# The output projection as a part of its own behind attention, by seven products for two row tiles, with contexts and gate through DRAM

## The chip, the core and the metric

The kernel runs on one core of one Trainium2 chip. The metric is the device time of one execution in microseconds, as the median of several runs. One more execution is recorded by the hardware profiler; its page and its trace give the durations used here. Engines are named as the profile names them: PE (matmul), PEld (weight loads of the matmuls), DVE (vector), ACT (scalar), POOL (GpSimd), SP (the queue that issues nearly all DMAs). "L738" is line 738 of the kernel.

## The reference, cut to what matters

```
x  = A_x                      # 1 x 2048 x 640, bfloat16
xn = layernorm(x)
q  = xn @ wq                  # 640 -> 32 heads x 192
k, v = the last 512 of 2048 cached positions, per head
o  = softmax(q k^T / sqrt(192)) @ v          # 32 heads, 2048 queries, 512 keys
s  = concat(o) @ wo           # 6144 -> 640
g  = silu((silu(xn @ w_gate) * (xn @ w_up)) @ w_down)   # 640 -> 1536 -> 640
out = x + s * g
```

Everything is bfloat16 in DRAM. There is no mask.

## The kernel before, in words

**Tiling.** The 2048 rows are 16 row tiles of 128, or 4 blocks of 512 (`NB`). Two heads make a pair (`NPAIR` = 16 pairs), 384 wide, which is three slices of 128. One (pair, block) is a step `i = pr * NB + b`. The order on every engine is written out by hand (the pools run under `manual_schedule`), so each engine executes its instructions in the order of the program, and a waiting instruction holds up all that stands behind it on its engine.

**First part.** Layernorm, and the gate branch (`ffn_hidden`, `ffn_down`), whose result `g` stays in SBUF in two layouts: columns 0 to 511 by row (`g_m`), columns 512 to 639 transposed (`g_t`). `x_transpose` keeps the same columns of x transposed in `xT`.

**Attention, pair by pair.** For each pair there are two halves of two blocks each. A half is a scores phase and a stretch.
- `scores_phase(pr, half)` has eight slots n. In each, `scores` makes S = k q for 128 keys, 512 queries and two heads (six matmuls of 64 rows by 512 columns; two row groups of 64 run side by side) and ACT takes the exponential (L601). Between them stand the products that make the q of a later half (`q_group`: `differences` at n = 0, `sides` at 1, `across` and `third(0)` at 3, `sums` at 4, `third(1)` at 6). `across` is a DVE instruction (L576) that must have read the PSUM tile before the matmuls of `sums` may add to it.
- `beside(pr, n)` puts loads and K work next to slot n, with n counted from 0 to 15 over both halves: `transpose_k(pr+1, kc)` (DMA transposes of the next pair's K, L167) at n = 0 to 3, `load_v(pr)` at 0, `load_wo(pr)` at 4, `sum_k` (DVE reductions over those transposes, L174) at 8 to 10, `load_k(pr+2)` at 11, `centre_k` at 12 to 15, `load_wq(pr+2)` at 15.
- The stretch multiplies the exponentials with V: `pv(i, q2)`, two units ("0a0" is block 0, rows 0 to 255, first turn) of 16 matmuls of 64 by 193 columns; between the two turns of one accumulator POOL writes a tiny tile (L725) that the second turn waits for. `divide` normalises the accumulators into `O_b` (DVE and ACT), and a DMA transpose (L655) turns `O_b` into `OT_b`, the context with its features on the partitions.
- Between the units of a stretch stand the output projection's units of the half before (`wo_units`): `wo_turn` (L738), row-tiled matmuls of 64 by 512 for columns 0 to 511, and `rest` (through `wo_rest`, L708) for columns 512 to 639 transposed. DVE adds each result to the running sums `s_m` and `s_t` in SBUF (`add_sum`, L751). So each pair's 384 features are projected as they come. The orders are three strings: `FIRST` (no projection yet), `LATER` and `LAST`.

**Pairs 14 and 15.** POOL multiplies the sums with g and adds x (L767, L778). Two of the four blocks of pair 14 are held back and projected together with pair 15's (`late`), and the last rows are finished in small pieces (`last_rows`, `wo_parts`, L833, L834) and stored.

**DMA.** SP issues in program order into one queue. Nothing that attention makes goes to DRAM before the output itself.

Of the kernel before, what the change touches and what calls it, by code (L numbers as in the profile page):

```python
# [15 lines left out]
def kernel(  # L16
# [34 lines left out]
    MC = D - P  # L51
# [14 lines left out]
    res = ctx.enter_context(tc.tile_pool(name="res", bufs=1))  # L66
    wpool = ctx.enter_context(tc.tile_pool(name="att_w", bufs=2))
    kpool = ctx.enter_context(tc.tile_pool(name="att_k", bufs=1))
    qpool = ctx.enter_context(tc.tile_pool(name="att_q", bufs=2))
    sc_pool = ctx.enter_context(tc.tile_pool(name="psum_sc", bufs=2, space=bass.MemoryType.PSUM))  # L70
# [14 lines left out]
    g_m = res.tile([P, T, MC], bf, name="g_m")  # L85
    g_t = res.tile([P, NB, 512], bf, name="g_t")
    xT = res.tile([P, NB, 512], bf, name="xT")

    NG = NB // 2
    DIFF, SUM, DIAG = 0, NG, 2 * NG  # L90
    xc = res.tile([P, 2 * NG + 1, NC, 512], h16, name="xc")

# [9 lines left out]
    V_p = consts.tile([P, KC, 2, Dh + 8], bf, name="V_p")  # L102
# [49 lines left out]
    def load_wo(pr):  # L152
        wo_p = pairs[pr]["wo"] = wpool.tile([P, 3, D], bf, name="wo_p")
        nc.sync.dma_start(
            out=wo_p[:], in_=wo[pr * PD : (pr + 1) * PD, :].rearrange("(j p) d -> p j d", p=P)
        )

# [40 lines left out]
    with ExitStack() as fctx:  # L201
        ffw = fctx.enter_context(tc.tile_pool(name="ffw", bufs=1))
        lnw = fctx.enter_context(tc.tile_pool(name="lnw", bufs=4))
        lnx = fctx.enter_context(tc.tile_pool(name="lnx", bufs=8))
        ffh = fctx.enter_context(tc.tile_pool(name="ffh", bufs=2))
        ffa = fctx.enter_context(tc.tile_pool(name="ffa", bufs=3))
# [124 lines left out]
        def x_transpose(t):  # L331
            nc.sync.dma_start_transpose(
                out=xT[:, t // 4, (t % 4) * P : (t % 4 + 1) * P], in_=x_t[t][:, MC:D]
            )

        def ffn_down(b, u):

            dn = mm_tile()[:, 0, :]
            to = g_m[:, 4 * b + u, :] if u < 4 else g_t[:, b, :]
            for f in range(NF):  # L340
                if u < 4:
                    at, by = hTs[b][:, f, u * P : (u + 1) * P], wd_sb[:, f, 0:MC]
                else:
                    at, by = wd_sb[:, f, MC:D], hTs[b][:, f, :]
                nc.tensor.matmul(dn, at, by, start=(f == 0), stop=(f == NF - 1))  # L345
            nc.scalar.activation(to, dn, ACT.Silu)
# [88 lines left out]
        mm_pool.append(ctx.enter_context(tc.tile_pool(name="psum_mm", bufs=1, space=bass.MemoryType.PSUM)))  # L435
# [4 lines left out]
        for b in range(NB):  # L440
# [4 lines left out]
            for f in range(NF):  # L445
# [13 lines left out]
                if f >= 8:  # L459
                    x_transpose(4 * b + f - 8)  # L460
# [17 lines left out]
                if b >= 1 and f in (1, 4, 6, 9, 11):  # L478
                    ffn_down(b - 1, u)
                    u += 1  # L480
                if b == 2:
                    if f == 0:
                        load_k(0)
                    elif 2 <= f < 6:
                        transpose_k(0, f - 2)
                    elif f == 6:
                        load_wq(0)
                    elif 7 <= f < 10:
                        sum_k(0, f - 7)
                elif b == 3:  # L490
                    if f < 5:
                        centre_k(0, f)
                    elif f < 8:
                        (load_k, load_wq, load_wo)[f - 5]((1, 1, 0)[f - 5])
        early_q = [(i, j) for i in range(2) for j in range(3)]
        for u in range(5):
            ffn_down(NB - 1, u)
            for _ in range((0, 1, 2, 2, 1)[u]):
                q_full(*early_q.pop(0))
            if xwork:  # L500
                xwork.pop(0)()
# [3 lines left out]
    sapool = ctx.enter_context(tc.tile_pool(name="sacc", bufs=1))  # L505
    ppool = ctx.enter_context(tc.tile_pool(name="att_p", bufs=10))
    opool = ctx.enter_context(tc.tile_pool(name="att_o", bufs=2))
    otpool = ctx.enter_context(tc.tile_pool(name="att_ot", bufs=3))
    smpool = ctx.enter_context(tc.tile_pool(name="att_sm", bufs=8))
    finp = ctx.enter_context(tc.tile_pool(name="fin", bufs=2))  # L510
    s_m = sapool.tile([P, T, MC], f32, name="s_m")
    s_t = sapool.tile([P, NB, 512], f32, name="s_t")
    m_f = sapool.tile([P, 2, 2, 512], f32, name="m_f")

    NS = NPAIR * NB
    turn_t = smpool.tile([P, 1], f32, name="turn_t", bufs=1)
    last = NPAIR - 1
    Ps, OTs, Obs, xbs = {}, {}, {}, {}


# [83 lines left out]
    def pv(i, q2):  # L604

        pr, b = divmod(i, NB)
        st = {}

        def part(p):
            if p == 0:  # L610
                if i not in OTs:
                    Obs[i] = opool.tile([P, 4, 2, Dh], bf, name="O_b")
                    tag = "OT_l" if late(i) and pr < last else "OT_b"
                    OTs[i] = otpool.tile([P, 12, P], bf, name=tag, tag=tag, bufs=2 if tag == "OT_l" else 3)
                st["acc"] = sc_tile() if i < 2 and q2 else mm_tile()
# [15 lines left out]
            if p == 3:  # L631
                divide(i, q2, acc, (0, 1) if q2 == i else (0,) if pr == last else ())
# [3 lines left out]
    def divide(i, q2, acc, by_dve):  # L636
        pr, b = divmod(i, NB)
# [4 lines left out]
        for k in range(2):  # L642
            qt = 2 * q2 + k
            a_k = a_v[:, k, :, :]
            if by_dve and k in by_dve:
# [14 lines left out]
    def pv_full(i, q2):  # L660

        pr, b = divmod(i, NB)
        if i not in OTs:
            Obs[i] = opool.tile([P, 4, 2, Dh], bf, name="O_b")
            tag = "OT_l" if late(i) and pr < last else "OT_b"
            OTs[i] = otpool.tile([P, 12, P], bf, name=tag, tag=tag, bufs=2 if tag == "OT_l" else 3)
        O_b, OT_b = Obs[i], OTs[i]
        acc = mm_tile()
        for k in range(2):
            qt = 2 * q2 + k  # L670
            for h in range(2):
                for kc in range(KC):
                    nc.tensor.matmul(  # L673
                        acc[:, k, h * 256 : h * 256 + Dh + 1],
                        Ps[i][kc][:, h, qt * P : (qt + 1) * P], V_p[:, kc, h, 0 : Dh + 1],
                        start=(kc == 0), stop=(kc == KC - 1),
                    )
        divide(i, q2, acc, ())

    def load_xb(b):  # L680

        xbs[b] = xc[:, (SUM, DIFF + 1, DIAG, DIFF)[b], :, :].rearrange("p c n -> p (c n)").bitcast(bf).rearrange(
            "p (t d) -> p t d", d=D
        )
        nc.sync.dma_start(
            out=xbs[b][:, :, MAIN],
            in_=x2[b * 512 : (b + 1) * 512, MAIN].rearrange("(t p) d -> p t d", p=P),
        )

    def rows(b, qts):  # L690

        t = slice(4 * b + qts.start, 4 * b + qts.stop)
        return s_m[:, t, :], g_m[:, t, :]

    def late(i):
        return i // NB >= NPAIR - 2 and i % NB >= 2

    def wo_cols(ps, i, qt, cols, first=True, end=True):
        for j in range(3):
            nc.tensor.matmul(  # L700
                ps, OTs[i][:, 3 * qt + j, :], pairs[i // NB]["wo"][:, j, cols],
                start=(first and j == 0), stop=(end and j == 2),
            )

    def wo_rest(ps, i, r=slice(0, P), first=True, end=True):

        for j in range(3):
            nc.tensor.matmul(  # L708
                ps.rearrange("p (t q) -> p t q", q=P), pairs[i // NB]["wo"][r, j, MC:D],
                OTs[i][:, :, :].rearrange("p (t j) q -> p j t q", j=3)[r, j, :, :],  # L710
                start=(first and j == 0), stop=(end and j == 2),
            )

    MAIN = slice(0, MC)

    def follows(m, earlier):
        tc.add_manual_dep(
            m.ins, earlier.ins.name,
            mybir.DependencyInfo(mybir.DependencyClass.Sync, mybir.DependencyReason.DATA),
            reason="row tiles change banks",  # L720
        )

    def turned(m, st):

        st["turn"] = nc.gpsimd.memset(turn_t[:], 0.0)  # L725
        follows(st["turn"], m)

    def after(m, st):
        if "turn" in st:
            follows(m, st.pop("turn"))  # L730

    def wo_turn(st, i, half, turn):

        ps = st["sc"]
        for j in range(3):
            for n, r in enumerate((lo, hi)):
                k = n ^ turn
                m = nc.tensor.matmul(  # L738
                    ps[:, k, :], OTs[i][r, 3 * (2 * half + k) + j, :],
                    pairs[i // NB]["wo"][r, j, MAIN],  # L740
                    start=(turn == 0 and j == 0), stop=(turn == 1 and j == 2), skip_group_check=True,
                )
                after(m, st)
        if turn == 0:
            turned(m, st)

    def add_sum(pr, to, ps):
        if pr == 0:
            nc.vector.tensor_copy(out=to, in_=ps)
        else:  # L750
            nc.vector.tensor_tensor(to, to, ps, ALU.add)  # L751

    def sum_rows(i, qts, sc):
        pr, b = divmod(i, NB)
# [272 lines left out]
```

## Time and profile before

| | |
|---|---|
| median of 3 runs | 912.74 us (912.26 to 912.97) |
| the profiled execution | 913.02 us, of which its instructions span 911.2 us |
| PE, DVE, ACT, POOL busy | 902.4, 585.6, 501.2, 149.0 us |
| granted PE clock | 1.000 |
| matmuls of the output projection | L738 x1296, L708 x354, L700 x144 |
| DMA | 81.98 MB, mean 90 GB/s |

The profile gives for each engine its busy time, and for each group of instructions of one line and shape their number, their busy time and the mean of one. Matmuls are pipelined: a matmul's "mean" is its way through the array, and what it costs in a row of others is the distance between two starts, which the timeline shows. A chain of waits is followed back from the last instruction: it says which engine was the limit in each stretch of time.

### The profile page before, as it was taken

The page shows a single profiled execution, that of the slowest core. Times are in us where ns is not written, and L with a number is a line of the kernel's source. Part 1 is how long each engine was busy: PE and PEld are TensorE (multiplying, and loading weights), DVE is VectorE, ACT ScalarE, POOL GpSimd, SP SyncE. Part 2 cuts the span into 40 slices and gives each one's busy share as a digit, 9 for nine tenths or more (in the row PEclk, how much of TensorE's full clock was granted, in tenths as well). Part 3 has the DMA queues.
Part 4 walks back from the last instruction along what each step waited for, and adds up shares of the span by engine and source line. Part 5 has one row for each costly group of instructions (what it writes and reads, how often), then busy time and mean ns, then how long its engine had stood idle before and what let it go on. Part 6 is the DMA issues. An engine that isn't in the chain of part 4 may idle for free.

```text
span 911.2 us, 23325 instructions
## 1 busy us (share of the span) xinstructions
PE 902.4 (99%) x9835; PEld 543.1 (60%) x9835; DVE 585.6 (64%) x862; ACT 501.2 (55%) x873; POOL 149.0 (16%) x299
## 2 busy tenths in 40 slices
PE   9999999999999999999999999999999999999988
PEld 5444444466666666666666666666666666665555
DVE  5443553365767676767676767676776767676767
ACT  4222222566656666666666666666565656565671
POOL 0000000011111111111111111111111111116746
PEclk9999999999999999999999999999999999999999
DMA  9414360044544544454445444444544554454435
GB/s 300 82 33 95 76 142 5 1 83 92 82 93 83 92 83 92 82 92 79 97 77 97 79 96 76 80 97 81 88 83 92 78 92 86 91 78 110 120 46 165
DMA packets 266025, 81.98 MB, mean 90 GB/s; under 512 B 244928, under 2 KB 265920, under 8 KB 265920
## 3 DMA queue, kind: packets, MB, share of 16 engines
q1 hardware_dynamic: 263552, 77.82, 43.5%
q10 hardware_dynamic: 2368, 2.67, 0.9%
q8 instruction: 77, 1.26, 0.6%
q14 instruction: 28, 0.23, 0.1%
HBM read 41.39 MB, written 2.62 MB: 48 GB/s over the span
## 4 chain that ended last, share of the span: by engine, by line
PE 94%; POOL 3%; issue 1%; DMA 1%; DVE 1%; ACT 0%; ACTq 0%; POOLq 0%
PE mm L622 17%; PE sc L597 16%; PE sc L738 15%; PE mm L543 12%; PE sc L315 11%; PE mm L529 7%; PE mm L345 6%; PE sc L708 4%; PE sc L700 2%; POOL s_m L778 1%; PE mm L673 1%; POOL s_m L767 1%; PE mm L700 1%; PE mm L352 1%; DMA x_t<-in_A_x_dram 1%
## 5 line engine op out<-in xcount | busy, mean ns | idle before, releaser
L601 ACT ACTIVATE p_t<-sc 128x1024 bf16<-128x1024 f32 x256 | 253.8, 1024 | 81.9 <-PE sc L597 81.7
L652 ACT ACTIVATE O_b<-mm,r 128x192 bf16<-128x192 f32 x490 | 166.0, 421 | 184.0 <-issue 110.4
L597 PE MATMUL sc<-qT,khat 64*128 64x512 bf16 x1536 | 197.6, 376 | 0.0
L622 PEld LDWEIGHTS <-p_t 64*128 64x128 bf16 x3744 | 166.4, 94 | 39.9 <-issue 2.9
L622 PE MATMUL mm<-V_p,p_t 64*128 64x193 bf16 x3680 | 186.9, 243 | 2.1 <-ACT O_b L652 1.1
L751 DVE TENSOR_TENSOR s_m<-s_m,sc 128x1024 f32<-128x1024 f32 x108 | 131.9, 1221 | 60.7 <-PE sc L738 52.9
L738 PE MATMUL sc<-wo_p,OT_b 64*128 64x512 bf16 x1296 | 169.1, 376 | 0.0
L597 PEld LDWEIGHTS <-khat 64*128 64x128 bf16 x1536 | 88.4, 94 | 75.7
L534 DVE TENSOR_REDUCE qT<-mm 128x512 bf16<-128x1024 f32 x66 | 80.8, 1224 | 32.8 <-PE mm L529 29.9
L751 DVE TENSOR_TENSOR s_t<-s_t,sc 128x512 f32<-128x512 f32 x108 | 74.2, 687 | 40.4 <-PE sc L708 38.5
L725 POOL MEMSET turn_t<- 128x1 f32 x225 | 22.1, 98 | 467.1 <-PE mm L622 282.4
L738 PEld LDWEIGHTS <-OT_b 64*128 64x128 bf16 x1296 | 70.3, 94 | 44.4 <-issue 0.3
L581 POOL TENSOR_TENSOR m_f<-m_f 128x1024 f32<-128x1024 f32 x28 | 65.7, 2348 | 177.8 <-DVE qT L576 171.5
L543 PE MATMUL mm<-xc,wq_p 64*128 64x512 f16 x750 | 94.4, 376 | 0.0
L543 PEld LDWEIGHTS <-wq_p 64*128 64x128 f16 (+1 forms) x1050 | 58.7, 94 | 54.5 <-issue 0.8
L529 PE MATMUL mm<-xnT,wq_p 64*128 64x512 bf16 x660 | 82.9, 376 | 1.0 <-DVE qT L534 0.9
L323 DVE TENSOR_TENSOR hT<-sc,sg 128x512 bf16<-128x512 f32 x46 | 31.7, 691 | 70.2 <-ACT sg L322 70.2
L322 ACT ACTIVATE sg<-sc 128x512 bf16<-128x512 f32 x46 | 27.3, 596 | 69.8 <-PE sc L315 69.8
L315 PE MATMUL sc<-xnT,wg_sb 128*128 128x512 bf16 (+1 forms) x260 | 60.3, 354 | 0.4 <-DMA wg_sb<-in_B_w_gate_dram 0.3
L576 DVE TENSOR_TENSOR qT<-mm,m_f 128x1024 bf16<-128x1024 f32 x30 | 36.7, 1224 | 37.2 <-ACT m_f L573 37.2
L315 PE MATMUL sc<-xnT,wu_sb 128*128 128x512 bf16 (+1 forms) x260 | 60.3, 355 | 0.3 <-DMA wu_sb<-in_B_w_up_dram 0.3
L529 PEld LDWEIGHTS <-wq_p 64*128 64x128 bf16 x660 | 36.0, 94 | 37.9 <-issue 6.5
(96 smaller groups left out, 717.1 us busy)
## 6 DMA issues: line engine op xcount, KB each, us to landing
wo_p<-in_A_wo_dram SPq DMA_DIRECT2D x16, 480.0 KB, 3.9
wq_p<-in_A_wq_dram SPq DMA_DIRECT2D x79, 80.0 KB, 2.9
K_p<-in_A_k_cache_dram SPq DMA_DIRECT2D x32, 192.0 KB, 3.0
V_p<-in_A_v_cache_dram SPq DMA_DIRECT2D x32, 192.0 KB, 3.1
wq_p<-in_A_wq_dram SPq DMA_DIRECT2D x90, 40.0 KB, 2.7
x_t<-in_A_x_dram SPq DMA_DIRECT2D x13, 160.0 KB, 3.0
xc<-in_A_x_dram SPq DMA_DIRECT2D x4, 512.0 KB, 4.1
OT_b<-O_b SPq DMA_TRANSPOSE x124, 2.8
```

Source lines behind the costliest of these rows:

```text
L315: nc.tensor.matmul(out, w_sb[:, c, f * P : (f + 1) * P], xnT[:, c, qc], start=(c == 0), stop=(c == NC - 1),)
L345: nc.tensor.matmul(dn, at, by, start=(f == 0), stop=(f == NF - 1))
L529: nc.tensor.matmul(q_ps[:, h, :], w[r, AS_IS[j], c, :], xnT[r, c, b * 512 : (b + 1) * 512], start=(c == 0), stop=(c == NC - 1),)
L534: nc.vector.reduce_sum(q_of(i, j), q_ps[:, :, :].rearrange("p h n -> p n h"), axis=AX.X)
L543: nc.tensor.matmul(ps[:, h, :], ws[h][r, c, :], xs[h][r, c, :], start=(first and c == 0), stop=(c == NC - 1), skip_group_check=True,)
L581: eng.tensor_tensor(m_f[:, SIDE_S, :, :], diag, m_f[:, SIDE_S, :, :], ALU.subtract)
L597: nc.tensor.matmul(sc[:, h, :], khat[r, j, ks], q_of(i, j)[r, :], start=(j == 0), stop=(j == 2))
L601: nc.scalar.activation(p_t[:, :, :], sc[:, :, :], ACT.Exp, scale=scale)
L622: m = nc.tensor.matmul(acc[:, k, h * 256 : h * 256 + Dh + 1], Ps[i][kc][r, h, qt * P : (qt + 1) * P], V_p[r, kc, h, 0 : Dh + 1], start=(p ...
L652: nc.scalar.activation(O_b[:, qt, h, :], a_k[:, h, 0:Dh], ACT.Copy, scale=r[:, k, h, :])
L738: m = nc.tensor.matmul(ps[:, k, :], OTs[i][r, 3 * (2 * half + k) + j, :], pairs[i // NB]["wo"][r, j, MAIN], start=(turn == 0 and j == 0), ...
L751: nc.vector.tensor_tensor(to, to, ps, ALU.add)
```

## The change

- The running sums, `wo_units`, `LATER` and all of the output projection inside attention are gone. A stretch now holds the V units alone (`CONTEXTS`, the order that `FIRST` was), with "a" units in the `mm` accumulators and "b" units in the `sc` tiles of the scores. DVE divides five of eight accumulator halves in a stretch, ACT three.
- `spill` writes each step's `OT_b` (384 KB) to a DRAM tile `o_d`, two per half, at slots 4 and 5 of the next scores phase. The gate is computed in one layout and written to `g_d`; `x_transpose` is gone.
- The projection is done afterwards for two row tiles at a time, (r, r + 4): the 2 x 2 blocks of A are the two row tiles by the two halves of the 6144 features, the 2 x 2 blocks of B the halves of `wo` by features and by columns. Strassen's M1 to M7 are seven products of 24 matmuls of 128 by 320 columns, for each of 8 row pairs. DVE forms five sums of A blocks for each row pair (`a_sum`, 128 by 3072, into float16) and all the sums of the products.
- The five sums of B blocks are made once, during pairs 0 to 12, by DVE (`wo_pieces`, `wo_sums`) and kept in DRAM (`wo_d`).
- At slot 0 of pair 14, SP issues the loads of three B operands (`load_b`, 1.97 MB each) and most of A's first row pair (`load_a`, 0.79 MB each when whole). The other four B operands are loaded behind pair 15's scores, where `res` and `wpool` are closed (`wide`). The order of the rest of pair 15 is the new `LAST`.

The diff, cut to its core:

```diff
@@ stretch and its orders
-    LATER = "0a0 0b0 0y0 0x0 0a1 0x1 0w0 0b1 0w1 1w0 1b0 1w1 1a0 1b1 1y0 1x0 1a1 1x1"
+    CONTEXTS = "0a0 0b0 0a1 0b1 1a0 1b0 1a1 1b1"
+    LAST = (
+        "0a0 s20 0b0 s21 0a1 s22 0b1 s23 1a0 s30 1b0 s31 1a1 s32 1b1 s33 "
+        "2a0 2b0 2a1 2b1 3a0 3b0 3a1 3b1"
+    )
+            units["%da" % k] = pv(i, 0, mm_tile, (0, 1) if k == 0 else (0,))
+            units["%db" % k] = pv(i, 1, sc_tile, (0,))
@@ beside
-        elif pr and n == KC:
-            load_wo(pr)
...
+        if prev >= 0 and n8 in (4, 5):
+            spill(prev + n8 - 4)
+        if pr < KH // 2:
+            if n == 9:
+                wo_pieces(pr)
+            elif n == 7 and pr:
+                wo_sums(pr - 1)
...
+        if pr == last - 1 and n == 0:
+            for m in EARLY:
+                load_b(m, pre)
+            for q in (2, 0):
+                load_a(0, q)
+            for q in (3, 1):
+                load_a(0, q, slice(0, KH - 6))
@@ the seven products
+    def product(n, m, ps, first=True, ns=1):
...
+            for c in range(KH):
+                nc.tensor.matmul(
+                    ps[k] if ns > 1 else ps, at[:, c, :], b_w[m][:, c, k * w : (k + 1) * w],
+                    start=(first and c == 0), stop=(c == KH - 1), skip_group_check=True,
+                )
...
+    def row_pair(n):
...
+        product(n, M6, Y)
+        a_sum(n, M5)
+        product(n, M3, Z)
...
+        product(n, M1, S1)
+        a_sum(n, M2)
...
+        product(n, M5, Z, first=False)
...
+        a_sum(n, M7)
+        product(n, M4, X)
...
+        if nxt:
+            a_sum(n + 1, M6)
+        product(n, M2, S2)
...
+        product(n, M7, X, first=False)
+        total(f1[:], X, f1[:])
+        finish(n, 0, 0, f1[:])
+        store(n, 0)
@@ the end of attention
+    scores_phase(last, 0)
+    actx.close()
+    wide = ctx.enter_context(tc.tile_pool(name="out_b", bufs=1, reuse_waits="tile"))
...
+    for q in (3, 1):
+        load_a(0, q, slice(KH - 6, KH - 3))
+    load_b(rest_b.pop(0), wide)
...
+            if name == "s31":
+                spill(i)
+                load_b(rest_b.pop(0), wide)
...
+            if name == "2a1":
+                spill(i + 1)
+                a_sum(0, M6)
+                for q in (1, 3):
+                    load_a(0, q, slice(KH - 3, KH))
+                load_b(rest_b.pop(0), wide)
+                load_xg(0)
+            elif name == "3a1":
+                spill(i + 2)
+                load_b(rest_b.pop(0), wide)
+    spill(i + 3)
...
+    a_sum(0, M1)
+    for q in (2, 0, 3, 1):
+        load_a(1, q)
+    for n in range(len(ROW_PAIRS)):
+        row_pair(n)
```

## The prediction, written before the changed kernel was run

> **What bounds the kernel now.** I read the page's chain of waits first, then the groups by line and shape, then the timelines of PE, SP and DVE over one pair, then windows over the first 25 us.
>
> ```profile
> PE 902.4 (99%) x9835; PEld 543.1 (60%) x9835; DVE 585.6 (64%) x862; ACT 501.2 (55%) x873; POOL 149.0 (16%) x299
> ...
> PE 94%; POOL 3%; issue 1%; DMA 1%; DVE 1%; ACT 0%; ACTq 0%; POOLq 0%
> ```
>
> PE is the limit throughout, and nothing else is near. So matmul columns removed are time removed, as long as nothing else takes PE's place. What a matmul costs in a row of others I take from starts. In the chain in order of time, 30 matmuls of 512 columns take 6.47 us, 215.7 ns each:
>
> ```profile
> 42.04 6.47 PE sc L315 x30
> ```
>
> In PE's timeline near the end, three of 256 columns take 0.33 us, 109.2 ns each. And in pair 0 the V units stand just as the new stretch has them, mm and sc in turn:
>
> ```profile
> 902.25 0.49 PE L700 MATMUL mm<-wo_p,OT_l 128*128 128x256 bf16 x3
> 902.58 0.49 PE L700 MATMUL mm<-wo_p,OT_b 128*128 128x256 bf16 x3
> ...
> 187.12 0.83 PE L622 MATMUL sc<-V_p,p_t 64*128 64x193 bf16 x16
> 187.79 0.83 PE L622 MATMUL mm<-V_p,p_t 64*128 64x193 bf16 x16
> 188.46 0.83 PE L622 MATMUL sc<-V_p,p_t 64*128 64x193 bf16 x16
> 189.12 1.24 PE L543 MATMUL mm<-xc,wq_p 64*128 64x512 f16 x10
> ```
>
> A unit every 0.667 us, with no gap, and the next phase follows at once: a stretch of eight is 5.33 us.
>
> **Matmuls removed and added.** L738 and L708 are 1620 row-tiled matmuls, two side by side, so 810 slots of 512; L708 and L700 have 126 whole ones and L700 48 of 256 columns (24 slots): 960 x 0.2157 = 207.1 us go. Seven products x 24 x 8 row pairs = 1344 matmuls of 128x320 come. Between the two rows above, 320 columns cost 109.2 + 64 x (215.7 - 109.2) / 256 = 135.8 ns, so 182.5 us (22.8 for a row pair). PE idles 2.9 us in pair 15's old order (windows 865 to 880), which go too. The tail from the last matmul's end to the end of the span is 4.0 us (907.2 to 911.2); the new one is one addition, two steps of `finish` and a store, some 4.6 by 0.49 + 2 x 0.6 us on DVE and 2.1 us to landing plus issue. Span without any new wait: 911.2 - 207.1 - 2.9 + 182.5 + 0.6 = **884.3 us**. That leaves 26.9 us for new waits before the gain is spent.
>
> **Attention without the projection.** A pair takes 46.1 us (V loads at 399.88 and 445.99) and loses 120 row-tiled matmuls, 12.9 us: 33.2. Does another engine need more? In that window DVE is busy 32.3 us: minus 16 additions (8 x 1.22 + 8 x 0.69 = 15.3), plus 10 divisions of 0.555 and, in 13 pairs, five sums of 0.486: 25.0. ACT 28.5 less 20 scalings of 0.421: 20.1. SP's issue time is 12 transposes of 1.21 to 1.4, 11 loads of wq 7.2, K and V 2.5, and new four spills and three `wo` DMAs of about 0.6: some 29 of 33. That is tight, so I followed SP through a half: the next V lands about 3 us before its first use. All three stay below PE. I take 2 us for small collisions; the bounds are 0 and 0.3 us for each of 29 halves, 9. DVE's work in the projection: the 16-bit sums of L372 take 680 ns at 1024 and 948 at 1536 elements, so 1.75 us at 3072; five of these, and 14 steps of 320 columns at 0.49 (one operand in PSUM) to 0.75 (float32 from SBUF, L581 scaled), make 16 to 19 us of 22.8. The row pair's 4.1 MB are 180 GB/s. So products run at PE's pace once they run. `ffn_down` keeps its columns; spills and `g_d` are behind nothing that PE waits for.
>
> **First new wait: K of pair 15.** SP issues in program order into one queue. SP's timeline around slot 0 of a pair (start, duration of the issue):
>
> ```profile
> 444.68 1.21 SPq L167 DMA_TRANSPOSE KT<-K_p  x1
> 445.99 1.26 SPq L147 DMA_DIRECT2D V_p<-in_A_v_cache_dram  x2
> 447.30 3.88 SPq L167 DMA_TRANSPOSE KT<-K_p  x3
> ```
>
> On DVE, the reductions over these transposes and the `across` behind them:
>
> ```profile
> 421.14 1.86 DVE L174 TENSOR_REDUCE ssum<-KT 128x1 f32<-128x512 bf16 x3
> 423.90 1.23 DVE L576 TENSOR_TENSOR qT<-mm,m_f 128x1024 bf16<-128x1024 f32 x1 [0.90 <-ACT m_f L573]
> ```
>
> In pair 14 the change puts 3 x 1.966 + 2 x 0.786 + 2 x 0.590 = 8.65 MB between the V loads and the last three K transposes. The first 25 us show what the queue does when it is full:
>
> ```profile
> 5.00:10.00 5.00, 4.11 (x49) 3.07 (x48) 3.47 (x12) 1.72 (x7) 0.00 (x0) 1.00 1.07 338
> 10.00:15.00 5.00, 5.00 (x93) 4.97 (x90) 2.24 (x8) 2.97 (x7) 0.00 (x0) 1.00 1.10 335
> 15.00:20.00 5.00, 5.00 (x34) 2.61 (x32) 3.87 (x9) 2.27 (x6) 0.00 (x0) 1.00 1.09 342
> ```
>
> The last column is GB/s. At 342 the 8.65 MB take 25.3 us. SP reaches them about 7 us into the phase (after four context transposes, one K transpose and V), so they end at 32.5, the three transposes behind them at 36.4. DVE reaches `sum_k` at slot 8 (11.7 + 5.3 = 17.0 us) and stops there; behind it on DVE stands `across` (L576), and PE may not start `sums` before `across`. PE gets to `sums` after two products of 1.08, one `third` of 1.08 and four scores of 0.65: at 22.8. It goes on at 36.4 + 1.86 + 1.22 + 0.2 = 39.7: **16.8 us** late. The new loads have runs of 4.6 to 15 KB, where before nearly all packets are under 2 KB, so the rate may be higher; no row shows it. At a fifth more I get 12.6. I take the middle, 14.7.
>
> The Trainium skill speaks to both points ("DMA: Bandwidth & Descriptors"). Its section "Queues, rings and completion order" has each DMA engine take descriptors in ring order, which is the rule against this change; the trace agrees in that 1.92 MB of w_down, issued behind the other loads, needed 11.6 us to land. Its section "Bandwidth" has 425 GB/s for 16 MB; an estimate by that figure makes the wait 12 us. No row here reaches it.
>
> **Second new wait: the way into the projection.** I count from the end of pair 15's scores phase. PE has 16 V units and 8 scores, 15.8 us, then M6, M3, M1 and so on, 3.26 us each. On SP stand, in order: the load of M5's B operand, transposes of block 0, its spill (which waits for them to land), the operand of M4, transposes of block 1, its spill, the last context pieces of row pair 0 (which wait for that spill), the operand of M2, four small loads, transposes of block 2, its spill, the operand of M7, the transpose of block 3, its spill, and only then row pair 1's contexts. Every 1.97 MB takes 5.2 to 5.8 us, a transpose lands 2.8 us after issue, a spill some 2.5 (160 KB need 2.1, 640 KB 3.6). Chained: block 0 landed 9.1, M4's operand moved by 17, block 1 landed 19.6, its spill done 22.4 (M1 could start at 22.4 without the wait, with it at 27), M2's operand 30.3, block 2 landed 33.8, M7's operand 42, block 3 landed 43.5, its spill done 46.3, two context tiles landed 52.6, the sum for M6 made 54.4. Row pair 1 would have started at 15.8 + 22.8 = 38.6. So **15.8 us**, with 13 and 19 as bounds for rates a fifth higher and lower. Later row pairs have a whole row pair's time for their loads.
>
> **Waking PE up.** Both waits leave PE idle for over 8 us. The trace shows what PE does after idleness only at the start:
>
> ```profile
> 1.23 4.66 PE L263 MATMUL gu<-zero_t 128*128 128x512 bf16 x15 [1.23 <-DVE zero_t L209]
> ```
>
> Nine of 512 and six of 128 columns, 5376 in all, take 4.5 us to the next start instead of 2.3. Gaps of 1 us near 873 and 876 cost nothing afterwards. So 0 to 2.2 us for each gap; I take 1.1, 2.2 for both. The skill's "TensorE: Matmul & The Clock Gate" (Part 1) says that an idle window of about 3.4 us halves the clock; by that it would be the whole 4.4.
>
> **The sum.** 884.3 + 2 + 14.7 + 15.8 + 2.2 = 919.0 us of span. The profiled execution was 913.02 for a span of 911.2, and 0.28 above the median, so against 912.74 that is 7.8 more: **920.5 us**, a little slower. The kernel saves 27 us of matmuls and waits 35 us for DMAs.
>
> **Rivals.**
> - *Faster: the queue does not hold up K.* If the transposes of pair 15's K pass the 8.65 MB, or these move much faster, the first wait goes with its waking: 919.0 - 14.7 - 1.1 = 903.2, time 905. With the second wait halved too, 895. It decides where both waits together fall below 25 us. For it: a 480 KB load among the first transfers landed in 7 us though the queue was full. Against it: that is just the time of what stood ahead.
> - *Slower by much: SP cannot feed attention in 33 us.* Its 29 us of issue leave 4; every spill waits for a transpose to land, and the wq loads then stand ahead of the next transposes. If V comes later than its 3 us of slack in each pair, say by 1.5, 14 pairs give 21 us: 941. Against it: no wait of PE on V in the trace, and SP idle for over 10 us of each pair.
> - *Products slower than 135.8 ns*, by sums of DVE that come late: 1 us for each of 56 products would give 976. DVE has 3 us to spare in each row pair, so I give it little.
>
> **How the numbers follow.** The forecast's own range is 910 to 932 (12.6 to 16.8, 13 to 19, 0 to 4.4, 0 to 9). I give both waits at about this size 0.62, the faster rival 0.24, slow attention 0.09, slow products 0.05. The range of 8 in 10 takes in most of the faster rival and reaches towards slow attention: 902 to 938. Differences under 0.2% (1.8 us) are no change here: the forecast's lower end lies there, so faster 0.26, same 0.08, slower 0.66.
>
> **What would show it.** Right: products at 136 ns starts, pairs 1 to 13 at 33 us; in pair 14 a wait of DVE at `sum_k` of over 12 us and PE idle behind it; PE idle before M1 of row pair 0 and by some 9 us before M6 of row pair 1; full speed after. Wrong: pairs of 35 us or more, or PE without a gap in pair 14.

## The result, and the profile after

| | before | after |
|---|---|---|
| median, in runs side by side | 912.62 us (4 runs) | 968.99 us (4 runs, 964.76 to 973.18) |
| profiled execution, its span | 913.02, 911.2 us | 964.76, 963.0 us |
| granted PE clock | 1.000 | 0.969 |
| DMA | 81.98 MB, 90 GB/s | 160.61 MB, 167 GB/s |

The ratio is 1.062 (1.057 to 1.066): the change costs 56 us, where the forecast was 8. The range ended at 938. The four executions of the changed kernel differ by 0.9%, those of the kernel before by 0.1%; the profiled one is the fastest, 4 us under the median.

The page's busy times, and the shares of the chain that ended last:

```profile
PE 897.9 (93%) x9688; PEld 586.3 (61%) x9705; DVE 565.5 (59%) x971; ACT 404.6 (42%) x577; POOL 82.9 (9%) x170
...
PE 72%; SPq 12%; DMA 11%; DVE 3%; issue 1%; ACT 0%; DVEq 0%; ACTq 0%
```

Before, PE alone carried 94% of the chain. Now nearly a quarter of it runs through SP's queue and DMAs. PE's busy time fell by 4.5 us only: a busy PE at half clock counts as busy.

**Where the time is.** The loads of V mark the pairs. In SP's timeline (start, duration of the issue), the four that bound pairs 1 to 12, 13 and 14:

```profile
214.67 1.25 SPq L154 DMA_DIRECT2D V_p<-in_A_v_cache_dram  x2
...
653.52 1.60 SPq L154 DMA_DIRECT2D V_p<-in_A_v_cache_dram  x2
685.33 1.26 SPq L154 DMA_DIRECT2D V_p<-in_A_v_cache_dram  x2
732.43 1.25 SPq L154 DMA_DIRECT2D V_p<-in_A_v_cache_dram  x2
```

Pairs 1 to 12 take (653.52 - 214.67) / 12 = 36.57 us where I had 33.2: 40 us in all. Pair 13, the only one of the fourteen with neither work on `wo` nor early loads, takes 31.8 between these marks, since SP makes up a delay there; on PE it takes 33.4 us (first products at 645.66 and 679.04), the length that was forecast. Pair 14 takes 47.1, with the wait that was forecast.

**What the long pairs look like.** One pair in SP's timeline, then DVE and PE at the start of the same pair (in brackets the idle time before an instruction and what ended it):

```profile
398.69 1.25 SPq L165 DMA_TRANSPOSE KT<-K_p  x1
400.03 1.26 SPq L154 DMA_DIRECT2D V_p<-in_A_v_cache_dram  x2
401.34 5.18 SPq L165 DMA_TRANSPOSE KT<-K_p  x3
406.56 1.13 SPq L663 DMA_DIRECT2D o_d<-OT_b  x2
408.52 0.36 SPq L706 DMA_DIRECT2D wo_d<-b_w  x1
409.67 7.01 SPq L654 DMA_TRANSPOSE OT_b<-O_b  x4
...
420.37 8.54 SPq L141 DMA_DIRECT2D wq_p<-in_A_wq_dram  x11
429.01 5.87 SPq L654 DMA_TRANSPOSE OT_b<-O_b  x4
434.93 1.25 SPq L165 DMA_TRANSPOSE KT<-K_p  x1
```

```profile
395.57 1.42 DVE L150 TENSOR_TENSOR wq_p<-wq_p 128x640 f16<-128x640 bf16 x3 [5.37 <-DMA wq_p<-in_A_wq_dram]
396.91 1.22 DVE L562 TENSOR_TENSOR qT<-mm,m_f 128x1024 bf16<-128x1024 f32 x1
```

```profile
398.18 1.86 PE L529 MATMUL mm<-xc,wq_p 64*128 64x512 f16 x10 [2.94 <-DVE qT L562]
399.80 2.62 PE L583 MATMUL sc<-qT,khat 64*128 64x512 bf16 x12
402.24 1.26 PE L515 MATMUL mm<-xnT,wq_p 64*128 64x512 bf16 x10
```

From one first K transpose to the next, 36.2 us, SP shows 34.0 us of groups with hardly a gap between them. The same groups were shorter in the trace of before: 3.88 us for three K transposes, here 5.18; 7.2 us for eleven loads of `wq`, here 8.54; context transposes as short as 1.21 each, here 7.01 for four. So `wq` of the next pair, the last in the queue, lands late. DVE stops at `combine_wq` (L150). `across` (L562) stands behind that on DVE, and PE may not start `sums` before `across`. Twelve of these waits, one in each of pairs 1 to 12, plus the 14.6 us in pair 14, are the 42.3 us that PE spends on "DVE qT L562".

Two windows give the mean share of the 16 DMA engines, the last column but one: from 222 to 403 us before, and over pairs 1 to 12 after.

```profile
222.00:403.00 181.00, 181.00 (x2300) 115.32 (x2297) 127.17 (x179) 111.72 (x198) 24.18 (x72) 1.00 0.46 86
...
214.70:653.50 438.80, 410.58 (x5542) 271.97 (x5540) 290.81 (x529) 261.94 (x360) 65.78 (x120) 0.97 0.80 177
```

The share goes from 0.46 to 0.80. The first busy time of a row is PE's: in pairs 1 to 12 it is idle for 438.80 - 410.58 = 28 us. That is 28 of the 40 us.

The idle time isn't the whole price; the other 12 us are slower work (granted clock 0.97 in that row). Three windows over that PE timeline; the column of the clock is the third from the end:

```profile
398.20:399.80 1.60, 1.60 (x11) 0.70 (x12) 1.06 (x1) 0.00 (x0) 1.59 (x1) 0.66 0.71 132
399.80:402.30 2.50, 2.50 (x16) 1.19 (x14) 1.22 (x1) 0.88 (x1) 0.75 (x1) 0.54 0.51 106
402.30:405.00 2.70, 2.70 (x28) 1.42 (x26) 1.23 (x1) 1.92 (x3) 0.00 (x0) 1.00 0.70 161
```

After a gap of 2.94 us PE works at about half clock for some 4 us. A product takes 1.62 us to the next start instead of 1.08, two scores 2.44 instead of 1.29: 1.7 us more for a gap of 3.

**The two waits that were forecast** are there, at their size. DVE and PE in pair 14:

```profile
713.73 1.87 DVE L172 TENSOR_REDUCE ssum<-KT 128x1 f32<-128x512 bf16 x3 [16.55 <-DMA KT<-K_p]
```

```profile
716.78 2.32 PE L529 MATMUL mm<-xc,wq_p 64*128 64x512 f16 x10 [14.57 <-DVE qT L562]
```

And PE on the way into the projection:

```profile
757.89 3.43 PE L749 MATMUL acc<-b_w,a_s 128*128 128x320 f16 x24
...
795.53 6.33 PE L749 MATMUL acc<-b_w,a_s 128*128 128x320 f16 x24 [6.62 <-DVE a_s L742]
...
811.48 3.42 PE L749 MATMUL acc<-b_w,a_q 128*128 128x320 f16 x24
814.74 3.56 PE L749 MATMUL acc<-b_w,a_s 128*128 128x320 bf16 x25
```

Row pair 1 starts at 795.53 and not at 757.89 + 22.8 = 780.7: 14.8 us late. After that, 24 matmuls take 3.26 us from start to start, 135.8 ns each.

### The profile page after: what moved, and what is told of

Same layout as the page of the kernel before. It is cut to its first block, busy times and chain, and to the rows that moved or that the text cites. A ratio compares the mean times of both kernels' runs of the same rounds, so it can differ in the third digit from the quotient of the medians.

```text
span 963.0 us, 23080 instructions
## 1 busy us (share of the span) xinstructions
PE 897.9 (93%) x9688; PEld 586.3 (61%) x9705; DVE 565.5 (59%) x971; ACT 404.6 (42%) x577; POOL 82.9 (9%) x170
## 2 busy tenths in 40 slices
DMA packets 319959, 160.61 MB, mean 167 GB/s; under 512 B 243056, under 2 KB 315120, under 8 KB 319216
## 4 chain that ended last, share of the span: by engine, by line
PE 72%; SPq 12%; DMA 11%; DVE 3%; issue 1%; ACT 0%; DVEq 0%; ACTq 0%
PE acc L749 17%; PE sc L583 13%; PE sc L313 10%; SPq L141 9%; PE mm L529 9%; PE mm L622 6%; PE mm L515 5%; PE mm L334 5%; PE sc L622 5%; DMA OT_b<-O_b 4%; DMA V_p<-in_A_v_cache_dram 2%; DMA wq_p<-in_A_wq_dram 2%; DVE qT L562 2%; DMA KT<-K_p 1%; DVE wq_p L150 1%
## 5 line engine op out<-in xcount | busy, mean ns | idle before, releaser
L583 PE MATMUL sc<-qT,khat 64*128 64x512 bf16 x1536 | 205.3, 388 | 0.0
L622 PEld LDWEIGHTS <-p_t 64*128 64x128 bf16 x4096 | 173.0, 94 | 14.6 <-issue 4.0
L749 PE MATMUL acc<-b_w,a_s 128*128 128x320 f16 (+1 forms) x960 | 139.8, 308 | 10.9 <-DVE a_s L742 8.7
L529 PE MATMUL mm<-xc,wq_p 64*128 64x512 f16 x750 | 99.7, 393 | 42.3 <-DVE qT L562 42.3
L749 PEld LDWEIGHTS <-a_s 128*128 128x128 f16 x960 | 96.2, 101 | 51.8 <-DVE a_s L742 9.3
L622 PE MATMUL mm<-V_p,p_t 64*128 64x193 bf16 x2176 | 115.3, 243 | 4.0 <-ACT O_b L651 2.5
L520 DVE TENSOR_REDUCE qT<-mm 128x512 bf16<-128x1024 f32 x66 | 80.7, 1223 | 36.7 <-PE mm L515 34.6
L622 PE MATMUL sc<-V_p,p_t 64*128 64x193 bf16 x1920 | 101.3, 243 | 0.1
L651 ACT ACTIVATE O_b<-sc,r 128x192 bf16<-128x192 f32 x120 | 43.9, 418 | 93.3 <-PE sc L622 43.5
L742 DVE TENSOR_TENSOR a_s<-a_q 128x3072 f16<-128x3072 bf16 x40 | 68.8, 1751 | 19.3 <-DMA a_q<-o_d 19.3
L515 PEld LDWEIGHTS <-wq_p 64*128 64x128 bf16 x660 | 36.6, 95 | 38.3 <-issue 7.9
L572 DVE TENSOR_TENSOR qT<-mm,m_f 128x1024 bf16<-128x1024 f32 x30 | 36.7, 1224 | 34.4 <-POOL m_f L567 29.8
L645 DVE TENSOR_TENSOR O_b<-mm,r 128x384 bf16<-128x384 f32 x102 | 53.7, 554 | 4.8 <-DMA OT_b<-O_b 2.3
```

Of the source, the lines that this page charges most:

```text
L515: nc.tensor.matmul(q_ps[:, h, :], w[r, AS_IS[j], c, :], xnT[r, c, b * 512 : (b + 1) * 512], start=(c == 0), stop=(c == NC - 1),)
L520: nc.vector.reduce_sum(q_of(i, j), q_ps[:, :, :].rearrange("p h n -> p n h"), axis=AX.X)
L529: nc.tensor.matmul(ps[:, h, :], ws[h][r, c, :], xs[h][r, c, :], start=(first and c == 0), stop=(c == NC - 1), skip_group_check=True,)
L583: nc.tensor.matmul(sc[:, h, :], khat[r, j, ks], q_of(i, j)[r, :], start=(j == 0), stop=(j == 2))
L622: m = nc.tensor.matmul(acc[:, k, h * 256 : h * 256 + Dh + 1], Ps[i][kc][r, h, qt * P : (qt + 1) * P], V_p[r, kc, h, 0 : Dh + 1], start=(p ...
L645: nc.vector.tensor_tensor(O_b[:, qt, :, :], a_k[:, :, 0:Dh], r[:, k, :, :].to_broadcast([P, 2, Dh]), ALU.mult,)
```

## Experiments

All were timed against the kernel before (medians 912.34 to 912.37 us). Two theories stood behind the first four: that only the place of a few DMAs in SP's order is wrong, and that SP has too much to do altogether.

**`wq` earlier in the queue.**

```diff
-        elif pr + 2 < NPAIR and n in (11, 15):
-            (load_k if n == 11 else load_wq)(pr + 2)
+        elif pr + 2 < NPAIR and n in (8, 11):
+            (load_k if n == 11 else load_wq)(pr + 2)
```

> SP issues the wq loads of pair pr+2 at slot 8 instead of slot 15, so ahead of the two wo pieces, K and the two spills and not behind them; bytes, DMAs and everything else are the same. Theory 1 (the order on SP makes wq late): the last wq load lands some 3.5 us earlier in each pair, DVE's wait at combine_wq (58.6 us in all, 14 times) falls under 15 us, PE's wait before sums goes, and with it the half clock that follows; pairs 1 to 13 fall from 36.6 to 33.2-33.8 us and the time by 35 to 44 us, to 925-935. Theory 2 (the DMA engines are full, whatever the order): the next thing in the queue is late instead (V or the K transposes), pairs stay above 35.5 us and the time above 955. The wait of 14.6 us in pair 14 and the 15 us before row pair 1 stay in both.

966.77 us (961.93 to 968.98), ratio 1.059 (1.055 to 1.062). The wait for `wq` is gone, but in the list of waits PE now stands before V (waited for, total, times, longest):

```profile
PEld L622 <- DMA V_p<-in_A_v_cache_dram: 30.8, 13, 4.0
PE mm L622 <- DMA V_p<-in_A_v_cache_dram: 25.9, 20, 3.5
```

Pairs 1 to 12 take (653.88 - 213.99) / 12 = 36.66 us, as long as before the edit. So it isn't the order: what stands last in the queue is late, whichever it is.

**The early loads of pair 14 behind the K transposes.**

```diff
-        if pr == last - 1 and n == 0:
+        if pr == last - 1 and n == 3:
```

> In pair 14 the 8.65 MB of early loads are issued at slot 3, behind the last of pair 15's K transposes, instead of slot 0, ahead of three of them. Theory (the queue holds up K): DVE's 16.6 us at sum_k and PE's 14.6 us behind it go. The loads now stand ahead of the context transposes of the next stretch, so O_b comes free some 36 us into the pair where the second stretch wants it at 30: a new wait of 3 to 6 us of PE. Net 9 to 14 us less, 955-960. Rival (the wait is bandwidth and only moves): the whole 14 us come back at O_b, time unchanged at 965-970.

959.63 us (958.10 to 964.14), ratio 1.052 (1.049 to 1.056): some 9 us less by the medians. The profiled execution is the slowest of its four (964.14); in its trace pair 14 takes 42.6 us instead of 47.1. The wait at `sum_k` is gone, and 9.8 us of it come back behind the context transposes, which the same 8.65 MB now hold up:

```profile
DVE O_b L645 <- DMA OT_b<-O_b: 14.6, 2, 11.8
...
PE mm L529 <- DVE O_b L645: 9.8, 1, 9.8
```

**Both edits.**

> Both edits. If the two waits are independent, the gains add: 45 to 58 us less than the changed kernel, 912-924, about the time of the kernel before. If they feed on the same resource, less than the sum.

961.83 us (957.60 to 967.08), ratio 1.056 (1.052 to 1.060). The waits for V (28.9 us) and for the context transposes (10.7 us of PE) are there together, those for `wq` and K are not. Nothing is gained over the second edit alone.

**K and the pieces of `wo` issued by ACT.**

```diff
-            nc.sync.dma_start(
+            (nc.scalar if pr > 1 else nc.sync).dma_start(
...
-            nc.sync.dma_start(
+            nc.scalar.dma_start(
```

The first place is in `load_k`, the second in `wo_pieces`.

> The wq loads stay at slot 15 and behind everything that they stood behind, but the K loads and the two wo pieces are issued by ACT instead of SP: same bytes, some 2.3 us less of SP's issue time ahead of wq in each pair. Theory 1 (SP's issue): wq lands about 2 us earlier, DVE's wait per pair falls from 4.2 to about 2, the pair from 36.6 to 34.0-35.0, the time by 20 to 33 us (936-949). Theory 2 (bytes in front of wq): the wait stays at 4 us and the time within 8 us of 969.

1035.37 us (1033.51 to 1038.42), ratio 1.135 (1.132 to 1.138): much slower, by none of the expected ways. ACT's timeline in one pair:

```profile
401.90 5.47 ACTq L691 DMA_DIRECT2D won<-in_A_wo_dram  x2
407.47 1.02 ACT L587 ACTIVATE p_t<-sc 128x1024 bf16<-128x1024 f32 x1 [6.49 <-DMA wq_p<-in_A_wq_dram]
```

Issuing two DMAs holds ACT for 5.5 us, until a `wq` load that SP issued has landed, and the exponentials that PE needs stand behind it. The reason is in the program: its DMAs use eight semaphores in turn, and each waits until the earlier user of its own semaphore, the eighth DMA before it, has landed. ACT's DMAs take turns with SP's. The same rule ties SP's pace to the time that DMAs need to land.

That led to theory B below: not the number of DMAs (theory A) but their bytes. Per pair the change adds 1.57 MB of spills and 1.47 MB for the sums of `wo`, and removes 0.49 MB.

**No work on `wo` in the pairs.** `wo_pieces` and `wo_sums` are taken out:

```diff
-        if pr < KH // 2:
-            if n == 9:
-                wo_pieces(pr)
-            elif n == 7 and pr:
-                wo_sums(pr - 1)
...
+        if 7 <= pr <= KH // 2:
+            if n == 9:
+                t = smpool.tile([P, 2, 16], bf, name="tiny", bufs=2)
+                for k in range(2):
+                    nc.sync.dma_start(out=t[:, k, :], in_=wo[k * P : (k + 1) * P, 0:16])
+            elif n == 7:
+                nc.sync.dma_start(out=t_d[:, :], in_=ident[:, 0:16])
```

> This kernel leaves out the work on wo inside the pairs (its loads, its sums, the write to wo_d); the B operands are read straight from wo, so the output is not the reference's. In pairs 7 to 12 three tiny transfers (4 KB each, two loads and one write) are issued in the places of the three that are gone; pairs 1 to 6 issue none. Theory A (the number of DMAs: SP's issue time and its waits are the whole limit): pairs 1 to 6 lose about 1.7 us of issue, 36.6 -> 34.9 us; pairs 7 to 12 lose nothing, 36.6 us; time about 950. Theory B (the bytes: writes to DRAM and loads of 1.47 MB per pair fill the 16 DMA engines, so that a transpose takes SP 1.9 us instead of 1.3): all of pairs 1 to 12 at 33.2 to 34 us, with or without the tiny ones, transposes back at 1.3 us; time 920 to 935. In pair 14 both expect the wait of DVE at sum_k to stay (15 to 22 us, the runs of the loads are shorter).

939.09 us (937.42 to 940.98), ratio 1.029 (1.028 to 1.031). SP's timeline, the loads of V in pairs 1, 7 and 13:

```profile
212.58 1.25 SPq L154 DMA_DIRECT2D V_p<-in_A_v_cache_dram  x2
...
413.02 1.25 SPq L154 DMA_DIRECT2D V_p<-in_A_v_cache_dram  x2
...
618.03 1.26 SPq L154 DMA_DIRECT2D V_p<-in_A_v_cache_dram  x2
```

Pairs 1 to 6: 33.4 us. Pairs 7 to 12, with three tiny DMAs each: 34.2. So of the 3.2 us that the work on `wo` costs a pair, its DMAs' number explains 0.8. The rest goes with their bytes or with DVE's five sums of 0.49 us, which this kernel leaves out too; the next run changes bytes alone. Median durations of the context transposes did not change (1.23 us in both kernels), so that part of theory B, slower issue of each transpose, is not what happens. What changes is the landing: K needs 3.1 us here, 4.7 with the work on `wo`, 2.9 in the kernel before.

**Spills of a third of the bytes in pairs 0 to 5.**

```diff
+        w = 3 if pr > 5 else 1
-        at = o_d[4 * b + qts.start : 4 * b + qts.stop, :, 3 * pr : 3 * pr + 3, :]
+        at = o_d[4 * b + qts.start : 4 * b + qts.stop, :, 3 * pr : 3 * pr + w, :]
...
```

> In pairs 0 to 5 each spill writes only the first of its three context chunks: as many DMAs, a third of the bytes (1.05 MB less per pair). The projection reads the chunks of pairs 6 to 13 twice in place of those of pairs 0 to 7, so the output is not the reference's. Pairs 6 to 13 are as in the changed kernel. Theory A (number of DMAs): pairs 1 to 5 as long as 7 to 12, 36.6 us; time as the changed kernel, 965. Theory B (bytes): pairs 1 to 5 at 34 to 35 us, pairs 7 to 12 at 36.6; time 953 to 960.

956.17 us (953.98 to 957.94), ratio 1.048 (1.046 to 1.050). The loads of V in pairs 1, 6, 7 and 13:

```profile
214.44 1.25 SPq L154 DMA_DIRECT2D V_p<-in_A_v_cache_dram  x2
...
389.03 1.26 SPq L154 DMA_DIRECT2D V_p<-in_A_v_cache_dram  x2
425.26 1.26 SPq L154 DMA_DIRECT2D V_p<-in_A_v_cache_dram  x2
...
644.47 1.59 SPq L154 DMA_DIRECT2D V_p<-in_A_v_cache_dram  x2
```

In one and the same run, pairs 1 to 5 take 34.9 us and pairs 7 to 12 36.5, with as many DMAs in the same order. The 1.05 MB are worth 1.6 us, or 2.2 against the same pairs of the changed kernel ((400.03 - 214.67) / 5 = 37.1). Bytes it is.

**Three operands that stay on the chip.** The sums for M6, M3 and M1 are made in the tiles that the projection reads; only M4's and M7's go to `wo_d`.

```diff
-            nc.vector.tensor_tensor(sums[:, 2 * k : 2 * k + 2, :], piece(x), piece(y), op)
+            k = LATE_SUMS.index(m) if m in LATE_SUMS else 0
+            to = sums[:, 2 * k : 2 * k + 2, :] if m in LATE_SUMS else b_w[m][:, 2 * n : 2 * n + 2, :]
+            nc.vector.tensor_tensor(to, piece(x), piece(y), op)
...
-            for m in EARLY:
-                load_b(m, pre)
```

> The sums of wo for M6, M3 and M1 are made in place in the tiles that the projection reads, so that only those of M4 and M7 go to wo_d: as many DMAs in each pair but 0.49 MB less written, and 5.9 MB less to load in pair 14. The whole computation is kept. Both theories: 2.8 MB of context loads before the last K transposes of pair 15 take 8 us, they are issued at 7+8+4 = 19 us, PE reaches sums at 22.8, so the wait at sum_k (16.6 us) and the half clock behind it go: -14 us. Theory A (number of DMAs): pairs unchanged at 36.6, 951 us. Theory B (bytes): a third of the surplus bytes gone, 1.1 us per pair, 14 in all: 937 us.

937.80 us (935.15 to 938.52), ratio 1.027 (1.026 to 1.029): 31 us faster than the changed kernel, at theory B's number. Pairs 1 to 12 take (640.01 - 213.23) / 12 = 35.6 us for 0.49 MB less, 12 us in all. Pair 14's wait shrinks from 14.6 to 2.5 us, another 12.

**The same, with M7's operand behind the contexts of row pair 1**, and the context loads of pair 14 at slot 3.

```diff
             elif name == "3a1":
                 spill(i + 2)
-                load_b(rest_b.pop(0), wide)
...
     for q in (2, 0, 3, 1):
         load_a(1, q)
+    load_b(rest_b.pop(0), wide)
```

> g1 with two more edits: the context loads of pair 14 stand behind the last K transposes (slot 3), and the load of M7's operand stands behind the contexts of row pair 1 instead of before them. Both theories: M7's 1.97 MB (5 to 6 us) leave the chain into row pair 1, so M6 of row pair 1 starts 9 us late instead of 15: 6 us less than g1. Theory A: 945. Theory B: 931.

936.57 us (934.11 to 937.59), ratio 1.026 (1.024 to 1.027): no measurable gain. PE now waits 16.3 us for M7's operand inside row pair 0 instead of waiting for the contexts behind it.

**The work on `wo` in the feed-forward stage**, and the early loads spread over pairs 11 to 14.

```diff
+                if b and f % 3 == 0:
+                    wo_pieces(4 * (b - 1) + f // 3)
+                elif b and f % 3 == 2:
+                    wo_sums(4 * (b - 1) + f // 3)
...
+        if last - 4 <= pr < last - 1 and n == 3:
+            load_b(EARLY[pr - last + 4], pre)
```

> All the work on wo (loads, sums, writes to wo_d) moves into the feed-forward stage, where the DMA share was 0.2 to 0.5 and DVE's busy share 0.3 to 0.5; the operands of M6, M3 and M1 are loaded in pairs 11, 12 and 13 (slot 3), the first contexts in pair 14 at slots 3 and 8. The computation is whole. Theory B (bytes in attention): pairs 1 to 10 at 33.4 us as without the work on wo, some 2 us more in the three pairs that load 1.97 MB each, no wait at sum_k in pair 14 (-14 us), feed-forward stage as long as before: 965 - 12 x 3.1 + 3 - 14 = 917 us (912 to 922). Rival: the cost comes along, since the feed-forward stage's own loads and DVE are held up by it: pair 0 starts 10 us or more later, time 927 or more.

931.11 us (923.57 to 934.98), ratio 1.022 (1.020 to 1.023); the profiled execution was the fastest of five, 923.57, so its trace does not show what the others lose. Its loads of V in pairs 1, 11 and 14:

```profile
222.44 1.25 SPq L154 DMA_DIRECT2D V_p<-in_A_v_cache_dram  x2
...
553.36 1.78 SPq L154 DMA_DIRECT2D V_p<-in_A_v_cache_dram  x2
...
663.37 1.83 SPq L154 DMA_DIRECT2D V_p<-in_A_v_cache_dram  x2
```

Pairs 1 to 10 take 33.1 us, the length that the prediction gave all of them. Pairs 11 to 13, each with one load of 1.97 MB, take 36.7. And part of the cost came along, as the rival had it: pair 1 is 7.8 us later, since DVE, waiting for the pieces of `wo`, makes PE wait. In DVE's and in PE's timeline:

```profile
135.41 0.49 DVE L451 TENSOR_TENSOR sums<-won 128x640 f16<-128x640 bf16 x1 [6.62 <-DMA won<-in_A_wo_dram]
```

```profile
138.88 0.59 PE L313 MATMUL sc<-xnT,wg_sb 128*128 128x512 bf16 x1 [4.48 <-DVE hT L321]
```

**The same, with row pair 1's contexts ahead of M7's operand and the last spills.**

```diff
-                load_xg(0)
-            elif name == "3a1":
-                spill(i + 2)
-                load_b(rest_b.pop(0), wide)
-    spill(i + 3)
...
     for q in (2, 0, 3, 1):
         load_a(1, q)
+    load_b(rest_b.pop(0), wide)
+    load_xg(0)
+    for k in (2, 3):
+        spill(i + k)
...
```

To make room, the tile `y` of `finish` has one buffer here instead of two.

> h2 with another order of SP at the way into the projection: the transposes of blocks 2 and 3 first, then the contexts of row pair 1, then M7's operand, then x and gate, and the spills of blocks 2 and 3 (which row pairs 0 to 3 don't read) last. The bytes before row pair 1 stay, less two spills. If it is the order behind waiting spills that makes row pair 1 15 us late, it comes within 3 to 9 us: 908 us (904 to 914). If it is the rate (13 MB of operands, contexts and transposes in 39 us), nothing is gained: 915 to 919.

932.00 us (926.48 to 934.48), ratio 1.020 (1.018 to 1.023): nothing gained. Windows (the last three columns are clock, DMA share, GB/s):

```profile
740.00:745.00 5.00, 5.00 (x39) 3.60 (x38) 0.00 (x0) 0.42 (x1) 0.00 (x0) 1.00 0.96 367
745.00:750.00 5.00, 0.83 (x7) 0.39 (x4) 0.00 (x0) 0.00 (x0) 0.00 (x0) 0.91 1.04 435
750.00:755.00 5.00, 0.00 (x0) 0.00 (x0) 0.43 (x1) 0.00 (x0) 0.00 (x0) 0.50 0.99 382
```

The DMA engines are full while PE stands. In this order that wait is the rate of the transfers: another order of the same bytes only moved it. It showed as DVE's wait of 14.7 us for the gate.

## Why the prediction was wrong

**The step that failed is "I take 2 us for small collisions", for attention.** Counted on PE, from the first product of pair 1 (205.17) to M6 of row pair 0 (757.89), it is 552.7 us. Fourteen pairs of 33.2 and 26.5 for pair 15 would be 491.3. Of the 61.4 us over that, the 14.6 of the first wait were forecast, with 1.1 for waking; 2 more were allowed; some 44 were not. That is all of the miss of the profiled execution: 963.0 - 919.0 = 44. (3 of the 44 us lie in pair 15, where PE waits twice for divisions by ACT; the median is 4 us longer still, which no trace here shows.) The term's upper bound was 9. The bounds given for the forecast's own range add up to 911 to 935 us, not to 910 to 932; 969 lies outside both.

The 29 us of 33 on SP were issue alone; with the waits inside the groups the trace shows 34.0 of 36.2. Two things were left out.
- *The DMA engines were not counted.* Before, they were busy 0.46 of the time, 21 us of a 46.1 us pair (0.50 in the pair from 399.88). The change adds 3.04 MB and takes 0.49 away; at the 342 GB/s that the prediction read from the first 25 us, this is 8.9 - 1.4 = 7.5 us more. That makes some 29 of 33.2 us, and it comes in bursts. The sum stood in the rows of before and wasn't made. Measured: 0.80 of 36.6 us, 29 us.
- *Landing times were taken from a queue with room.* Spills were put at 2.5 us and landed in 4.3; K at 2.9 before landed in 4.7. SP's next DMAs wait for them, so what was "idle for over 10 us of each pair" was used up. The waits of PE that follow are short (0.9 to 4.9 us) but come in every pair, and behind half of them the clock is halved too.

**The rival "slower by much" had the place and the sign.** It put 1.5 us into each pair and named V; it was 3.4 us, and `wq` came late first (V took its place when `wq` was moved). At 3.4 us for 12 pairs its 941 would have been 961. With 0.09 it had far too little weight for a queue with 4 us to spare.

**First wait: right, with some luck in the number.** 14.6 us for 14.7. Windows there show 423 GB/s from 690 to 700 and 395 from 700 to 710, so near the upper of the two rates between which I took the middle (342 and 410), for which I had worked out 12.6; why it was 2 us more I did not take apart. The Trainium skill gives 425 GB/s for a transfer of 16 MB issued from GpSimd ("DMA: Bandwidth & Descriptors", Bandwidth). That figure is all but reached here, by loads with long runs that SP issues. The experiments say more than the size: taken out of K's way, 8.65 MB stop the context transposes instead (9.8 us), and only fewer bytes remove the wait (2.5 us).

**Second wait: right in size, the mechanism in part.** 14.8 us for 15.8, counted from M6 of row pair 0; counted as the prediction did, from the end of pair 15's scores phase (738.82), row pair 1 starts at 56.7 us instead of 54.4. What I called a chain of orders and spills is mostly a matter of rate: two other orders gained nothing. The chain is there as well: from 783 to 788 us, while the last transpose and spill land, the changed kernel's DMA share is 0.42.

**Products: right.** 135.8 ns measured, 135.8 worked out. DVE's sums take 1.75 us, and the steps of 320 columns 0.48 to 0.49, also from float32 in SBUF, the lower end of what I had.

**Waking PE up: the mechanism right, the number of times wrong.** I counted two gaps. The two cost 1.4 us (after 14.57 us idle) and 2.9 (after 6.62) where I took 1.1 each, and there are fourteen more: two of 2 us inside row pair 0 and one in each of pairs 1 to 12. Among those twelve, after gaps of 2.02, 2.35, 2.76, 2.94, 3.36 and 4.91 us PE was slow for some 4 to 5 us; after 0.87, 1.16, 1.37, 1.53, 2.06 and 2.42 us nothing was lost. The skill says that the clock is halved after an idle window of about 3.4 us ("TensorE: Matmul & The Clock Gate", Part 1). Here four gaps of 2.0 to 2.9 us were enough.

**What stays open.** How the 3.4 us of a pair divide between full DMA engines and the waits of each DMA for the eighth before it: fewer bytes relieve both, and no run changes only the second. And whether the best version so far can get below the kernel before. It has 19 us to go by its median; its trace, 7.5 us under the median, shows some 10 us in pairs 11 to 13, 8 us in the feed-forward stage and 14 us before row pair 1. A version that loads the operands in pairs 0 and 14, and has PE make M6, M3 and M1 of both first row pairs while the other operands come, was not run.

## What to carry to other kernels

When work is taken off the limiting engine and its data sent through DRAM, add up the DMA engines' busy time for one period as carefully as PE's, since here a queue at nearly 0.9 of a period (29 of 33.2 us), moving in bursts, was already the limit. If a transfer that is late stops being late after a reordering and another takes its place, stop reordering and count bytes. And price a short PE gap with its clock: a gap of 2.94 us cost nearly 5.

## What the runs showed of the hardware that I had not expected

- In attention each MB costs 1.5 to 2.0 us of a pair (1.6 us for 1.05 MB of spills, 1.0 for 0.49 MB of `wo_d`, 3.5 for a load of 1.97 MB), though the mean DMA share is only 0.77 to 0.82. The spills alone cost nothing: pairs 1 to 10 with the work on `wo` moved ahead of them take 33.1 us, at a share of 0.75.
- Gaps of PE between 2.0 and 2.9 us halve its clock afterwards in some cases (2.02, 2.35, 2.76, 2.94 us) and not in others (2.06, 2.42 us).
- Loads with runs of 4.6 to 15 KB (B operands and contexts) reach 423 to 435 GB/s over 5 to 10 us; the loads of the first 25 us reach 342, in a kernel whose packets are nearly all under 2 KB.
- Two DMAs issued by ACT held it for 5.5 us, because they took turns with SP's DMAs on the same semaphores. The skill says that DMAs of several issuing engines share the same 16 DMA engines, and that issuing on several only saves issue time ("DMA: Bandwidth & Descriptors", Issuing engines are not separate DMA queues). Here it did not save even that: 1035 us instead of 969.
